# C-B products of a unit in one step, over two PSUM banks, in a fused scan and two-MLP kernel

## The chip, the cores and the metric

The kernel runs on one core of one Trainium2 chip. The metric is the device time of one execution, in microseconds (us). Engines are named as in the profile: PE (TensorE, the matrix engine), DVE (VectorE), ACT (ScalarE), POOL (GpSimd) and SP (the engine whose queue issues the DMAs).

## What is computed

A scan in chunks feeds a first MLP, and that a second one. The scan has 4 batches, 8 heads, 768 steps, head size 32 and state size 16; each MLP takes the 3072 x 256 result as its tokens.

```
for c in range(nc):
    cum = np.cumsum(la, axis=-1)
    L = np.exp(cum[:, :, :, None] - cum[:, :, None, :]) * causal
    CB = np.einsum('bhin,bhjn->bhij', Cc, Bc)
    y_intra = np.einsum('bhij,bhjd->bhid', CB * L, xc)
    y_inter = np.einsum('bhin,bhnd->bhid', Cc, state) * decay_to_i[:, :, :, None]
    y[:, :, sl] = y_intra + y_inter
    state = decay_full[:, :, None, None] * state + np.sum(Bx, axis=2)
x = y as tokens x 256
h = x @ w_in;  g = where(h > 0, h, exp(min(h, 0)) - 1);  x = g @ w_out     (d_ff 2048)
out = ((x @ w_a) * (x @ w_b)) @ w_out                                      (d_ff 1536)
```

## The kernel before

**Units and tiles.** The scan is cut into 24 units (`unit`, L556): one chunk of 128 steps of one batch, all 8 heads. Four units make a tile of 512 tokens; there are six tiles. Units 0 to 3 feed tile 0, units 4 to 7 tile 1, and so on. The first MLP runs tile by tile, in 8 pairs of hidden blocks a tile (`pair`, `down`); the second MLP runs in 18 groups after it (`group`), as products of seven sums over two tiles.

**What a unit does.** DVE turns the decay row into the triangle L by two scans (`scan`, L630), one for each half of the heads. PE makes the C-B products, one 128 x 128 product per head with 16 rows of contraction (`cbm`, L683; for units 0 to 3 `cbm2`, L666). DVE multiplies them into L (`mask`, L686), one instruction per half. PE then makes y (`ym`, L717, L721) and the change of state (L725). ACT and DVE read y out of its bank: `x_hi` and `x_lo` (L760, L763), or `x_w` for tile 0, and `st_up` (L741) for the state.

**How the C-B products stand.** In units 0 to 3 the two halves of the heads lie on two groups of rows of PE (partitions `row` and `row + 32`), in f32; `cbm2` issues all eight products in one step, from one group and the other in turn, and writes into two banks of a ring. Units 4 to 7 have the same f32 data, units 8 to 23 have bf16 data that is cut into three parts and stacked over 128 rows. In units 4 to 23 a unit has two steps of four products, both into the bank `cbank`, so the second waits for the first half's mask:

```
i_cb = add({"PE": 0.28 if s else 0.88}, cbm, cb.take(), i_sm, due=due, ...)
...
i_k = add({"DVE": 0.685}, mask, i_cb, i_scan[g], i_le, due=due)
```

**Banks.** PSUM has eight banks: two for each of the two `up` buffers, two `acc`, `cbank` and `ybank`. `ybank` holds y in columns 0 to 255 and two buffers for the change of state (`dsb`) in 256 to 383. Products on zeros go to 384 to 511.

**What sets the order.** Every piece of work is a step handed to `Plan.add` with its cost on an engine, the steps it follows and a due time. `Plan.emit` (L156 on) walks through them with a clock of its own, takes the step with the earliest start and then the earliest due time, and writes it to its engine's queue. The order on all engines is fixed when the program is made. `MOVE` is a table that shifts due times of single steps by hand. Until 50 us of that clock, where PE would stand still, the planner has `warm` write products on zeros (`plan.fill`, L369) into its queue; below they are called fills.

**Weights.** They come as 64-bit floats and are turned to f32 by ACT, DVE and POOL (`weight`). Tile 0 is multiplied in plain f32 (`whole_mm`, L783); from tile 1 on every operand is split in a high and a low part, with three products for one (L792 to L795, L804 to L808).

Of the kernel before, what the change touches and what calls it, by code (L numbers as in the profile page):

```python
# [17 lines left out]
P = 128  # L18
NB, NH, S, D, N = 4, 8, 768, 32, 16
# [27 lines left out]


MOVE = {
    ("bc", (0, 2, 1)): {"": 3.2, "rest": -2.7},  # L50
    ("bc", (1, 2, 0)): {"rest": 2.4},
    ("late", 1): {"rest": -2.9},
    ("late", 3): {"": -1.4, "comb": 1.7, "high_s": 3.6},
    ("late", 4): {"": 2.6, "high": 2.5},
    ("late", 6): {"": -5.0, "comb": 3.2},
    ("late", 8): {"": -20},
    ("pair", (1, 3)): {"": -2.5},
    ("pair", (3, 3)): {"": -1.3},
    ("pair", (3, 5)): {"": 1.0},
    ("pair", (3, 6)): {"": 0.6},  # L60
    ("pair", (4, 0)): {"": -2.1},
    ("split", ("w_in", 2)): {"": -4.1},
    ("split", ("w_in", 3)): {"": 5.8},
    ("split", ("w_out", 0)): {"high": -1.3},
    ("split", ("w_out", 1)): {"high": 5.2},
    ("split", ("w_out", 3)): {"": -1.3},
    ("unit", 0): {"scan": -2.0},
    ("unit", 1): {"ld_x": 2.0},
    ("unit", 10): {"": 5.1, "ld_x": -0.4, "x_lo": -0.4},
    ("unit", 11): {"st_up": 0.1},  # L70
    ("unit", 12): {"": 7.3, "ld_sm": 1.4, "mask": 4.4},
    ("unit", 13): {"": -3.7},
    ("unit", 14): {"ld_sm": -1.5},
    ("unit", 15): {"": 1.6, "<lambda>": -1.2, "xend": 4.0, "ym": 4.4},
    ("unit", 16): {"cbm": 0.8, "st_bd": 1.3},
    ("unit", 17): {"x_lo": 4.1},
    ("unit", 18): {"<lambda>": -5.5},
    ("unit", 19): {"cbm": 0.5},
    ("unit", 2): {"scan": -0.3},
    ("unit", 20): {"": -4.2, "<lambda>": -1.0, "st_bd": -1.1},  # L80
    ("unit", 21): {"": 7.1, "mask": -5.0, "scan": 2.8},
    ("unit", 22): {"": 2.7, "ld_sm": -1.6, "ld_x": 1.7},
    ("unit", 23): {"": 1.9, "ld_a": 2.0, "scan": 1.7},
    ("unit", 3): {"cbm": 2.6, "last_col": 3.1, "mask": -0.9},
    ("unit", 4): {"": 1.9, "cbm": -3.5, "mask": 0.4},
    ("unit", 5): {"x_lo": -2.4},
    ("unit", 7): {"": 1.6, "ym": -2.8},
    ("unit", 9): {"": -3.0, "st_up": -3.3},
    ("w", ("w_in", 0)): {"sign": -1.0},
    ("w", ("w_in", 2)): {"put": -2.4},  # L90
    ("w", ("w_in", 3)): {"load": -1.7},
    ("w", ("w_out", 1)): {"sign": -0.6},
    ("w", ("w_out", 2)): {"": 2.4},
    ("wb", ("w_a", 0)): {"last3": -1.1},
    ("wb", ("w_a", 1)): {"": 7.0},
    ("wb", ("w_a", 2)): {"load": -5.3, "scale": 3.3, "sign": 0.4},
    ("wb", ("w_b", 2)): {"": 2.4},
    ("wb", ("w_out2", 1)): {"": 3.2, "put": 4.0, "shift": -3.9},
    ("wb", ("w_out2", 2)): {"": 6.1, "shift": 1.8},
    ("xset", 1): {"": 11.1},  # L100
    ("xset", 2): {"": 10.6, "f_t3": -8.8, "x_h": 1.6, "x_l": 6.0},
}


# [133 lines left out]
def kernel(  # L238
# [14 lines left out]
    nc = tc.nc  # L253
# [71 lines left out]
    cbank = psum.tile([P, 4, P], F32, name="cbank", tag="cbank")  # L325
# [3 lines left out]
    cbb, yb = Buf(cbank), Buf(ybank)  # L329
    accb = [Buf(a) for a in accs]  # L330

    def flat4(bf):
        return bf.ap.rearrange("p h i -> p (h i)") if len(bf.ap.shape) == 3 else bf.ap
# [7 lines left out]
    plan = Plan()  # L341
# [214 lines left out]
    def unit(u, due):  # L556
# [82 lines left out]
        if c < NCH - 1:  # L639
# [15 lines left out]
            i_xe = add({"POOL": 0.71}, xend, i_le, i_p, xe.take(), due=due, port=True)  # L655
            xe.users.append(i_xe)
            le.users += [i_le, i_xe]
        i_cbs = None
        if n == 0:

            def cbm2(e):
                for h in range(4):
                    for g in range(2):
                        q = slice(h * P, (h + 1) * P)
                        t = sm32[row + 32 * g:row + 32 * g + N]
                        nc.tensor.matmul(flat4(cb_[g])[:, q], t[:, 0, q], t[:, 1, q], start=True, stop=True)  # L666

            i_cbs = add({"PE": 0.95}, cbm2, cb_[0].take(), cb_[1].take(), i_sm, due=due, weight=0.25)
            smu.users.append(i_cbs)
        for g in range(2):  # L670
            h4 = slice(4 * g, 4 * g + 4)

            cb = cb_[g] if n == 0 else cbb

            def cbm(e, g=g, cbank=cb.ap):
                for h in range(4):
                    if s == 0:
                        q = slice(h * P, (h + 1) * P)
                        t = sm32[row + 32 * g:row + 32 * g + N]
                    else:  # L680
                        q = slice((4 * g + h) * P, (4 * g + h + 1) * P)
                        t = sm.ap
                    nc.tensor.matmul(cbank[:, h, :], t[:, 0, q], t[:, 1, q], start=True, stop=True)  # L683

            def mask(e, h4=h4, cbank=cb.ap if len(cb.ap.shape) == 3 else cb.ap.rearrange("p (h i) -> p h i", h=4)):
                nc.vector.tensor_mul(lt[:, h4], cbank, lt[:, h4])  # L686

            if n:
                i_cb = add({"PE": 0.28 if s else 0.88}, cbm, cb.take(), i_sm, due=due, pad=pd, weight=1.0 if s else 0.125)
                smu.users.append(i_cb)  # L690
            else:
                i_cb = i_cbs
            i_k = add({"DVE": 0.685}, mask, i_cb, i_scan[g], i_le, due=due)
            cb.users += [i_cb, i_k]
            i_msk.append(i_k)
        i_cd = i_sbd = None
        if c > 0:
# [99 lines left out]
    def down(ph, t, f, gh, gl, i_h, i_l, due):  # L797

        name = "w_out" if ph == "A" else "w_out2"
        last = (NA if ph == "A" else NBF) - 1  # L800
        wk = (name, f // 4)

        def hi_mm(m, first):
            nc.tensor.matmul(accs[m], w_mm(name, whi, f, m), gh, start=(f == 0), stop=False)  # L804
            nc.tensor.matmul(accs[m], w_mm(name, wlo, f, m), gh, start=False, stop=False)  # L805

        def lo_mm(m):
            nc.tensor.matmul(accs[m], w_mm(name, whi, f, m), gl, start=False, stop=(f == last))  # L808

        def dn_h(e):  # L810
            hi_mm(0, f == 0)
            hi_mm(1, f == 0)

        def dn_l(e):
            lo_mm(0)
            lo_mm(1)

        def dn_0(e):
            hi_mm(0, False)
            lo_mm(0)  # L820

        def dn_1(e):
            hi_mm(1, False)
            lo_mm(1)

        prev = i_down.get((ph, t))
        d = (accb[0].take() + accb[1].take()) if f == 0 else prev
        if ph == "A" and t == 0:
            i1 = []
            for m in range(2):  # L830
                def dn_w(e, m=m):
                    whole_mm(accs[m], name, f, m, gh, f == 0, f == last)

                i1.append(add({"PE": 0.86}, dn_w, i_h, i_m[wk], d, i1, due=due))
            i_down[ph, t] = i1
            mbuf[wk].users += i1
            return i1, i1
        if f < last:
            i1 = add({"PE": 4 * MM}, dn_h, i_h, i_hi[wk], i_lo[wk], d, due=due)
            i2 = add({"PE": 2 * MM}, dn_l, i_l, i1, due=due)  # L840
            i_down[ph, t] = i2
            w_used[wk] += [i1, i2]
            return [i1, i2], [i2, i2]
        i1 = add({"PE": 3 * MM}, dn_0, i_h, i_l, i_hi[wk], i_lo[wk], d, due=due)
        i2 = add({"PE": 3 * MM}, dn_1, i1, due=due)
        w_used[wk] += [i1, i2]
        return [i1, i2], [i1, i2]

    def pair(t, p):
# [14 lines left out]
        for q, k in ((q, k) for q in range(2 if t == 0 and p < NHALF else 0) for k in range(2)):  # L864

            def up_h(e, k=k, f=2 * p + k, q=q):
                o = slice(q * 256, (q + 1) * 256)
                for c in range(2):
                    whole_mm(u[:, k, o], "w_in", f, c, x0[:, c, o], c == 0, c == 1)

            i_u.append(add({"PE": 0.88}, up_h, d_u, i_u, i_x[t][2 * q:2 * q + 2], i_m["w_in", 0],
                           due=due + 7.0 * q + 0.1 * k))
            mbuf["w_in", 0].users.append(i_u[-1])
        for k in range(0 if t == 0 and p < NHALF else 2):
            f = 2 * p + k

            def up_a(e, k=k, f=f):
                up_mm(u[:, k, :], "w_in", f, t)

            wk = ("w_in", f // 4)  # L880
            if t == 0:
                i_u.append(add({"PE": 1.72}, up_a, d_u, i_u, i_x[t], i_m[wk], due=due + 0.1 * k))
                mbuf[wk].users.append(i_u[-1])
            else:
                i_u.append(add({"PE": 6 * MM}, up_a, d_u, i_u, i_x[t], i_hi[wk], i_lo[wk], due=due + 0.1 * k))
                w_used[wk].append(i_u[-1])
# [551 lines left out]
```

## Time and profile before

| what | value |
|---|---|
| three runs, median | 628.99 us (628.84 to 629.89) |
| the profiled execution, its own time | 627.92 us |
| its span, from the first to the last instruction | 626.2 us |
| PE busy | 619.4 us (99%) |
| DVE, ACT, POOL busy | 392.6, 372.4, 342.8 us |
| moved by DMA | 59.96 MB, mean 96 GB/s |
| TensorE clock granted, mean | 0.998 |

The profile is of one execution. What lies around its span, 1.7 us, is start and end of the program. In its table of f32 products one product in the program is two records in the trace, since PE passes twice; bf16 products and those on split operands have one record. The duration printed for a record on PE contains the way through the array, so records overlap; what a product costs in a full queue is the distance from its start to the next start.

### The profile page before, as it was taken

Reading aid. Unit: us, or ns where it says so; the run is one execution under the profiler, and the core shown is the slowest. Engines: PE = TensorE matmul, PEld = TensorE weight load, DVE = VectorE, ACT = ScalarE, POOL = GpSimd, SP = SyncE. Lnnn points to the kernel's source line nnn. Section 1 sums busy time; section 2 is a strip of 40 time slices with the busy share of each in tenths; the row PEclk is TensorE's granted clock in tenths of the full one; section 3 lists DMA queues with packets and bytes.
Section 4 is the critical chain, followed back from the end, with each engine's and each line's share of the span. In section 5 each row is a group of like instructions: output and inputs, shape, how many; then the busy total and the mean of one; then the engine's idle time right before and its main releaser. Section 6 shows DMA issues by size and latency. Waiting matters only on the chain. (4 is left out here: it accounts for less than half of the span.)

```text
span 626.2 us, 9495 instructions
## 1 busy us (share of the span) xinstructions
PE 619.4 (99%) x3658; PEld 485.3 (77%) x3658; DVE 392.6 (63%) x525; ACT 372.4 (59%) x528; POOL 342.8 (55%) x260
## 2 busy tenths in 40 slices
PE   9999999999999999999999999999999999999997
PEld 8955556788777788777888888888888888788885
DVE  7876686787876987887753766346533446433333
ACT  2375747647676776756678655557544456554443
POOL 2233465246764586546637476557655666555552
PEclk9999999999999999999999999999999999999999
DMA  6968622657668766410000000000100000100001
GB/s 194 337 198 268 208 66 92 223 173 269 214 201 299 269 211 188 152 51 1 1 1 0 2 0 1 0 1 1 68 0 2 2 0 1 68 2 0 1 0 68
DMA packets 33405, 59.96 MB, mean 96 GB/s; under 512 B 2736, under 2 KB 13904, under 8 KB 33360
## 3 DMA queue, kind: packets, MB, share of 16 engines
q1 hardware_dynamic: 33360, 59.35, 28.9%
q8 instruction: 29, 0.48, 0.3%
q14 instruction: 16, 0.13, 0.1%
HBM read 47.61 MB, written 11.73 MB: 95 GB/s over the span
## 5 line engine op out<-in xcount | busy, mean ns | idle before, releaser
L1209 DVE TENSOR_TENSOR x<-x 128x512 f32<-128x512 f32 x36 | 31.7, 884 | 82.5 <-POOL x L1253 82.0
L911 POOL TENSOR_TENSOR gl<-e,gh 128x1024 fp32r<-128x1024 f32 x20 | 50.9, 2545 | 29.1 <-ACT gh L904 21.9
L1215 POOL TENSOR_TENSOR gl<-x,gh 128x512 fp32r<-128x512 f32 x35 | 48.8, 1395 | 32.9 <-ACT gh L1212 32.9
L1253 POOL TENSOR_TENSOR x<-e,x 128x512 f32<-128x512 f32 x36 | 46.3, 1304 | 31.6 <-ACT e L1192 29.4
L804 PE MATMUL acc<-gh,hi_w_out 128*128 128x512 f32 x160 | 63.4, 396 | 0.0
L805 PE MATMUL acc<-gh,lo_w_out 128*128 128x512 f32 x160 | 62.4, 390 | 0.0
L890 ACT ACTIVATE e<-up 128x1024 f32<-128x1024 f32 x44 | 45.1, 1024 | 26.2 <-PE up L795 18.8
L630 DVE TENSOR_TENSOR_SCAN ab<-ab,delta 128x512 f32<-128x512 f32 x36 | 53.6, 1514 | 0.0
L808 PE MATMUL acc<-gl,hi_w_out 128*128 128x512 f32 x160 | 51.3, 397 | 0.1
L894 ACT ACTIVATE e<-e,bias 128x1024 f32<-128x1024 f32 x44 | 50.7, 1153 | 1.0
L900 DVE SCALAR_TENSOR_TENSOR up<-e,up 128x512 f32<-128x512 f32 x40 | 27.7, 692 | 24.8 <-ACT e L894 24.1
L1215 POOL TENSOR_TENSOR gl<-p,gh 128x512 fp32r<-128x512 f32 x18 | 23.9, 1327 | 30.8 <-issue 25.9
L792 PE MATMUL up<-xh,hi_w_in 128*128 128x512 f32 x96 | 39.4, 410 | 0.6 <-DVE gl L909 0.6
L1200 DVE TENSOR_TENSOR p<-acc,p 128x512 f32<-128x512 f32 x36 | 24.6, 690 | 24.5 <-PE acc L1182 23.2
L900 DVE SCALAR_TENSOR_TENSOR e<-e,up 128x512 f32<-128x512 f32 x48 | 30.7, 679 | 11.6 <-ACT e L894 11.4
L1121 PE MATMUL up<-gh,lo_w_out 128*128 128x512 f32 x96 | 37.5, 391 | 0.0
L793 PE MATMUL up<-xh,lo_w_in 128*128 128x512 f32 x96 | 37.5, 390 | 0.0
L1120 PE MATMUL up<-gh,hi_w_out 128*128 128x512 f32 x96 | 37.4, 390 | 0.0
L493 POOL TENSOR_TENSOR m<-m,raw 128x1024 int32<-128x1024 int32 x10 | 26.0, 2605 | 16.9 <-DVE m L483 13.9
L805 PEld LDWEIGHTS acc<-gh,lo_w_out 128*128 128x128 f32 x160 | 30.1, 188 | 5.9
L804 PEld LDWEIGHTS acc<-gh,hi_w_out 128*128 128x128 f32 x160 | 30.0, 188 | 5.9
L686 DVE TENSOR_TENSOR ab<-cbank,ab 128x512 f32<-128x512 f32 x37 | 25.3, 683 | 13.4 <-PE cbank L683 12.6
(306 smaller groups left out, 1731.9 us busy)
## 6 DMA issues: line engine op xcount, KB each, us to landing
ab<-a_seg SPq DMA_DIRECT2D x18, 512.0 KB
parts<-raw SPq DMA_DIRECT2D x64, 128.0 KB
sm<-parts SPq DMA_DIRECT2D x16, 512.0 KB
p<-in_xb SPq DMA_DIRECT2D x20, 256.0 KB
raw<-in_w_out SPq DMA_DIRECT2D x4, 1024.0 KB
fx<-in_w_out SPq DMA_DIRECT2D x3, 1024.0 KB
out_t<-m SPq DMA_DIRECT2D x12, 256.0 KB
raw<-in_w_in SPq DMA_DIRECT2D x2, 1024.0 KB
```

The lines of the kernel that those rows point to most:

```text
L630: nc.vector.tensor_tensor_scan(lt[:, h4].rearrange(flat), lt[:, h4].rearrange(flat) if n else flat4(sp[g]), delta.rearrange(flat), 0.0, op ...
L792: nc.tensor.matmul(ps, w_mm(name, whi, f, c), xh[:, c, :], start=(c == 0), stop=False)
L793: nc.tensor.matmul(ps, w_mm(name, wlo, f, c), xh[:, c, :], start=False, stop=False)
L804: nc.tensor.matmul(accs[m], w_mm(name, whi, f, m), gh, start=(f == 0), stop=False)
L805: nc.tensor.matmul(accs[m], w_mm(name, wlo, f, m), gh, start=False, stop=False)
L808: nc.tensor.matmul(accs[m], w_mm(name, whi, f, m), gl, start=False, stop=(f == last))
L890: nc.scalar.activation(gf, u, AF.Exp)
L894: nc.scalar.activation(gf, gf, AF.Identity, bias=bias[:, 0:1])
L900: nc.vector.scalar_tensor_tensor(u[:, k, :] if on_dve else gf[:, k, :], gf[:, k, :], 0.0, u[:, k, :], op0=ALU.min, op1=ALU.max)
L911: nc.gpsimd.tensor_sub(gl.ap, gf, gh.ap.bitcast(F32))
L1215: eng[e].tensor_sub(tap("l" + w), tap(wa), tap("h" + w).bitcast(F32))
L1253: eng[e].tensor_add(tap(w), tap(v), tap(w))
```

## The change

It touches the C-B products of units 4 to 23, and the due times.

- A unit's eight C-B products become one step. The first half goes to `cbank`, the second to `ybank`, over all its 512 columns. So the step waits until the y, and both buffers of the change of state, of the unit before have been read out.
- Units 4 to 7 now take the form of units 0 to 3 (`cbm2`): products of the two row groups in turn. Units 8 to 23 keep one product after the other, eight in a row (`cbm`).
- Both masks wait for the one step; the second reads `ybank`.
- With unit 4's C-B step the fills end, as `ybank` is no longer free for them.
- `MOVE` is written anew, from 52 to 104 entries, and the planner's costs of the f32 products of tile 0 go up. The costs are seen by the planner alone.

```diff
 MOVE = {
-    ("bc", (0, 2, 1)): {"": 3.2, "rest": -2.7},
...
+    ("bc", (0, 1, 0)): {"": 2.5, "load": 0.9},
...
-        i_cbs = None
-        if n == 0:
-
-            def cbm2(e):
+
+        if n:
+            cb_ = [cbb, yb]
+        cap = [flat4(x) for x in cb_]
+
+        def cbm2(e):
+            if n:
+                plan.fill = None
+            for h in range(4):
+                for g in range(2):
+                    q = slice(h * P, (h + 1) * P)
+                    t = sm32[row + 32 * g:row + 32 * g + N]
+                    nc.tensor.matmul(cap[g][:, q], t[:, 0, q], t[:, 1, q], start=True, stop=True)
+
+        def cbm(e):
+            for g in range(2):
                 for h in range(4):
...
+                    q = slice((4 * g + h) * P, (4 * g + h + 1) * P)
+                    nc.tensor.matmul(cap[g][:, h * P:(h + 1) * P], sm.ap[:, 0, q], sm.ap[:, 1, q], start=True, stop=True)
+
+        old = cb_[0].take() + cb_[1].take() + (dsb[0].users + dsb[1].users if n else [])
+        if s == 0:
+            i_cb = add({"PE": 1.1 if n == 0 else 1.25}, cbm2, old, i_sm, due=due, weight=0.25)
+        else:
+            i_cb = add({"PE": 0.58}, cbm, old, i_sm, due=due, pad=pd)
+        smu.users.append(i_cb)
...
-                i1.append(add({"PE": 0.86}, dn_w, i_h, i_m[wk], d, i1, due=due))
+                i1.append(add({"PE": 0.92}, dn_w, i_h, i_m[wk], d, i1, due=due))
...
-            i_u.append(add({"PE": 0.88}, up_h, d_u, i_u, i_x[t][2 * q:2 * q + 2], i_m["w_in", 0],
+            i_u.append(add({"PE": 0.92}, up_h, d_u, i_u, i_x[t][2 * q:2 * q + 2], i_m["w_in", 0],
...
-                i_u.append(add({"PE": 1.72}, up_a, d_u, i_u, i_x[t], i_m[wk], due=due + 0.1 * k))
+                i_u.append(add({"PE": 1.84}, up_a, d_u, i_u, i_x[t], i_m[wk], due=due + 0.1 * k))
```

How it moves instructions is shown at two places of PE's queue. The first is unit 4, while tile 0 is in the first MLP. Before (`sm_76` holds B and C, `x_93` tile 0, `m_104` and `m_103` weights, `e_86` a result of the hidden layer):

```order
L783 MATMUL up_115<-x_93,m_104 128x512 x2
L683 MATMUL cbank<-sm_76 128x128 x4
L783 MATMUL up_115<-x_93,m_104 128x512 x2
L783 MATMUL acc_117<-e_86,m_103 128x512
L783 MATMUL acc_118<-e_86,m_103 128x512
L717 MATMUL ybank<-p_74,sbd 32x128 x4
L721 MATMUL ybank<-f_hi_w_out_99,p_74 32x128 x4
L717 MATMUL ybank<-p_74,sbd 32x128 x4
L721 MATMUL ybank<-f_hi_w_out_99,p_74 32x128 x4
L725 MATMUL ybank<-xe,p_74 32x64 x4
```

This is unit 4's second half and then its y; the first half stands six products earlier, behind unit 3's y. Now:

```order
L722 MATMUL cbank<-sm_76 128x128
L722 MATMUL ybank<-sm_76 128x128
L722 MATMUL cbank<-sm_76 128x128
L722 MATMUL ybank<-sm_76 128x128
L722 MATMUL cbank<-sm_76 128x128
L722 MATMUL ybank<-sm_76 128x128
L722 MATMUL cbank<-sm_76 128x128
L722 MATMUL ybank<-sm_76 128x128
L832 MATMUL up_115<-x_93,m_104 128x512 x4
L766 MATMUL ybank<-p_74,sbd 32x128 x4
L770 MATMUL ybank<-f_hi_w_out_99,p_74 32x128 x4
```

All eight products stand together, the two banks in turn, four f32 products of the MLP ahead of unit 4's y; where the first half stood, behind unit 3's y, there are now 18 fills.

The second place is unit 8's y in tile 1, still on PE (`gh_90` and `xh_608` are operands of the first MLP). Before:

```order
L717 MATMUL ybank<-p_74,sbd 32x128 x4
L721 MATMUL ybank<-ab_78,p_74 32x128 x4
L725 MATMUL ybank<-xe,p_74 32x64 x4
L683 LDWEIGHTS sm_77
L683 MATMUL cbank<-sm_77 128x128
L683 LDWEIGHTS sm_77
L683 MATMUL cbank<-sm_77 128x128
L683 LDWEIGHTS sm_77
L683 MATMUL cbank<-sm_77 128x128
L683 LDWEIGHTS sm_77
L683 MATMUL cbank<-sm_77 128x128
L804 MATMUL acc_117<-gh_90,hi_w_out_862 128x512
```

Unit 9's first half follows unit 8's y at once; this is so behind 12 of the 16 y steps of units 8 to 23. Now:

```order
L766 MATMUL ybank<-p_74,sbd 32x128 x4
L770 MATMUL ybank<-ab_78,p_74 32x128 x4
L774 MATMUL ybank<-xe,p_74 32x64 x4
L841 MATMUL up_115<-xh_586,hi_w_in_824 128x512
L842 MATMUL up_115<-xh_586,lo_w_in_832 128x512
L841 MATMUL up_115<-xh_586,hi_w_in_824 128x512
L842 MATMUL up_115<-xh_586,lo_w_in_832 128x512
L844 MATMUL up_115<-xl_590,hi_w_in_824 128x512 x2
L853 MATMUL acc_117<-gh_90,hi_w_out_837 128x512
```

Here products of the MLP follow, 16 of 512 columns until unit 9's C-B step. Over the whole program PE has 190 fills before and 176 now; its other products are the same in number.

## Rows read from the trace of the kernel before

**Rows 1.** The page, parts 1 and 2: PE busy (first line), its granted clock in tenths

```profile
PE 619.4 (99%) x3658; PEld 485.3 (77%) x3658; DVE 392.6 (63%) x525; ACT 372.4 (59%) x528; POOL 342.8 (55%) x260
...
PEclk9999999999999999999999999999999999999999
```

**Rows 2.** Who waited for whom, PE: total us, times, longest; without the start

```profile
PE up L792 <- DVE gl L909: 0.6, 1, 0.6
PE up L1124 <- POOL gl L1215: 0.4, 1, 0.4
PE cbank L683 <- DVE ab L686: 0.2, 1, 0.2
```

**Rows 3.** PE's timeline (start us, duration us, engine, line), unit 0's C-B step

```profile
7.29 0.37 PE L666 MATMUL cbank<-sm 16*128 16x128 f32 x1
7.30 0.37 PE L666 MATMUL up<-sm 16*128 16x128 f32 x1
...
8.38 2.05 PE L606 MATMUL acc<-a,delta 128*128 128x128 f32 x16
```

**Rows 4.** PE's timeline around a C-B step of unit 6 and one of unit 7

```profile
61.63 3.60 PE L783 MATMUL up<-x,m 128*128 128x512 f32 x8
65.16 1.15 PE L683 MATMUL cbank<-sm 16*128 16x128 f32 x8
66.24 1.12 PE L783 MATMUL acc<-m,m 128*128 128x512 f32 x2
67.21 1.88 PE L783 MATMUL up<-x,m 128*128 128x512 f32 x4
...
80.11 2.74 PE L783 MATMUL acc<-e,m 128*128 128x512 f32 x6
82.78 1.15 PE L683 MATMUL cbank<-sm 16*128 16x128 f32 x8
```

**Rows 5.** PE's timeline, the longest row of fills, then unit 3's y

```profile
25.52 4.35 PE L369 MATMUL ybank<-zt 128*128 128x128 bf16 x75
29.80 0.65 PE L721 MATMUL ybank<-f_lo_w_out,f_lo_w_out 128*32 128x128 f32 x16
```

**Rows 6.** PE's timeline, a bf16 C-B step behind unit 8's y

```profile
120.82 0.40 PE L683 MATMUL cbank<-sm 128*128 128x128 bf16 x4
121.03 0.48 PE L804 MATMUL acc<-gh,hi_w_out 128*128 128x512 f32 x1
121.34 0.40 PE L805 MATMUL acc<-gh,lo_w_out 128*128 128x512 f32 x1
```

**Rows 7.** Timeline of all engines: unit 8's y step ends and is read out

```profile
120.59 0.29 PE L725 MATMUL ybank<-xe,p 128*32 128x64 f32 x8
...
120.96 0.37 ACT L760 CAST xh<-ybank 128x256 fp32r<-128x256 f32 x1
...
121.36 0.28 DVE L741 SCALAR_TENSOR_TENSOR state<-state,db,ybank 128x64 f32<-128x64 f32 x1
121.56 0.42 DVE L763 TENSOR_TENSOR xl<-ybank,xh 128x256 fp32r<-128x256 f32 x1
...
121.89 0.68 DVE L686 TENSOR_TENSOR ab<-cbank,ab 128x512 f32<-128x512 f32 x1
```

**Rows 8.** Busy time in a stretch: its length, then PE, weight load, DVE, ACT, POOL

```profile
110.00:290.00 180.00, 179.13 (x1395) 142.10 (x1394) 143.02 (x195) 122.74 (x149) 103.50 (x77) 1.00 0.59 195
```

**Rows 9.** PE's timeline around the longest wait

```profile
202.00 0.39 PE L804 MATMUL acc<-gh,hi_w_out 128*128 128x512 f32 x1
202.23 0.39 PE L805 MATMUL acc<-gh,lo_w_out 128*128 128x512 f32 x1
202.46 0.61 PE L808 MATMUL acc<-gl,hi_w_out 128*128 128x512 f32 x2
203.70 0.47 PE L792 MATMUL up<-xh,hi_w_in 128*128 128x512 f32 x1 [0.63 <-DVE gl L909]
```

**Rows 10.** PE's timeline, the first product of tile 1

```profile
92.61 0.79 PE L792 MATMUL up<-xh,hi_w_in 128*128 128x512 f32 x1
```

More of the change, by code (lines that the diff above doesn't have):

```diff
@@ L49 @@
 MOVE = {
-    ("bc", (0, 2, 1)): {"": 3.2, "rest": -2.7},
[L51 to L101, printed above, removed]
[7 rows of a table added]
+    ("group", 10): {"dn_h": -1.9, "mm3": -0.6},
+    ("group", 11): {"": -3.2},
+    ("group", 12): {"dn_l": 3.4, "mm3": 1.3},
+    ("group", 17): {"mm3": -4.2},
+    ("group", 2): {"dn_l": -1.5, "mm3": 2.2},
+    ("group", 4): {"lo": -2.8},
+    ("group", 5): {"": -5.2, "ad": 7.0},
@@ new lines @@
+    ("group", 9): {"": -8.9},
+    ("late", 2): {"": 12.6, "high": 4.0},
+    ("late", 3): {"": 6.7, "comb": -4.6, "high": 9.3},
+    ("late", 4): {"high": -7.5, "rest": -5.3},
+    ("late", 5): {"": -20, "high": 7.7},
+    ("late", 6): {"": -8.9},
+    ("late", 7): {"": 16.7},
+    ("late", 8): {"": -5.4, "high": -5.6},
+    ("pair", (0, 2)): {"em": -4.7},
+    ("pair", (0, 3)): {"dn_w": 4.5, "gg": -10.0},
+    ("pair", (0, 4)): {"": -0.9},
+    ("pair", (0, 7)): {"dn_w": 6.1},
+    ("pair", (1, 0)): {"": -1.5},
@@ new lines @@
+    ("pair", (1, 2)): {"": 3.9, "dn_h": 2.3},
+    ("pair", (1, 3)): {"": 1.2},
+    ("pair", (1, 6)): {"": 2.9},
+    ("pair", (1, 7)): {"up_a": -0.9},
+    ("pair", (2, 0)): {"": 0.7, "gg": 3.7},
+    ("pair", (2, 1)): {"lo": 3.6, "up_a": -4.1},
+    ("pair", (2, 2)): {"": 3.7, "dn_h": -1.4, "dn_l": -4.5, "hi": 1.2, "up_a": -2.7},
+    ("pair", (2, 3)): {"": -1.3, "em": 1.9, "up_a": -3.0},
+    ("pair", (2, 4)): {"dn_l": 4.0},
+    ("pair", (2, 5)): {"": -4.9, "hi": -3.2},
+    ("pair", (2, 6)): {"": -7.9, "up_a": -0.9},
@@ new lines @@
+    ("pair", (2, 7)): {"": 0.7},
+    ("pair", (3, 0)): {"": -0.3, "lo": 5.1},
+    ("pair", (3, 2)): {"": 3.3, "em": 0.3, "up_a": 0.8},
+    ("pair", (3, 3)): {"": -4.6, "dn_l": 1.6},
+    ("pair", (3, 4)): {"up_a": 1.4},
+    ("pair", (3, 5)): {"": -1.9, "dn_h": 8.0},
+    ("pair", (3, 7)): {"dn_l": 3.9, "up_a": 2.9},
+    ("pair", (4, 0)): {"": 9.2},
+    ("pair", (4, 1)): {"lo": -1.4},
+    ("pair", (4, 3)): {"": -15.6},
+    ("pair", (4, 4)): {"": -1.1, "dn_h": -2.2, "dn_l": -0.5},
+    ("pair", (4, 5)): {"": 13.1, "dn_h": -1.2},
@@ new lines @@
+    ("pair", (5, 0)): {"dn_l": 4.4, "up_a": 2.8},
+    ("pair", (5, 2)): {"dn_h": -1.1},
+    ("pair", (5, 3)): {"dn_l": 1.0},
+    ("pair", (5, 4)): {"": 6.3, "dn_l": 2.7, "up_a": 2.2},
+    ("pair", (5, 5)): {"": 0.9, "dn_h": -2.1, "dn_l": 5.5},
+    ("pair", (5, 7)): {"dn_h": -0.2},
+    ("split", ("w_in", 0)): {"": 3.9},
+    ("split", ("w_in", 1)): {"": -4.0, "rest": 3.8},
+    ("split", ("w_in", 2)): {"high": -0.9},
+    ("split", ("w_in", 3)): {"": 6.6, "high": 2.6},
+    ("split", ("w_out", 0)): {"high": 7.8, "rest": 7.2},
@@ new lines @@
+    ("split", ("w_out", 2)): {"": -15.8},
+    ("split", ("w_out", 3)): {"": -3.7, "high": 6.3},
+    ("unit", 0): {"": -10.0, "ld0": 2.0, "ld_x": 9.0, "x_w": 3.5},
+    ("unit", 1): {"": -3.1, "scan": -4.0},
+    ("unit", 11): {"st_up": 1.2},
+    ("unit", 12): {"<lambda>": 8.7, "mask": -15.0},
+    ("unit", 13): {"": -12.8, "<lambda>": 5.6, "scan": 1.4},
+    ("unit", 14): {"": 1.6, "cbm": 5.9, "x_hi": -5.2},
+    ("unit", 15): {"ld_a": -2.0, "ld_x": -0.9, "scan": 5.1, "x_hi": 2.9},
+    ("unit", 16): {"": -6.3, "cbm": 17.1, "last_col": -10.8, "ld_x": 17.3, "xend": -10.4},
@@ new lines @@
+    ("unit", 17): {"": 3.1, "last_col": -20, "ld_a": 14.1, "st_bd": 4.7, "xend": 1.1},
+    ("unit", 18): {"": -1.7, "<lambda>": -5.9, "ld_a": 4.1, "ld_sm": 19.2, "scan": 2.9, "st_bd": 4.4},
+    ("unit", 19): {"": 11.0, "ld_sm": 7.3, "scan": -6.6, "ym": 11.5},
+    ("unit", 2): {"": 12.1},
+    ("unit", 20): {"": -1.8, "mask": 9.6, "scan": -2.0},
+    ("unit", 21): {"": -4.0, "scan": 7.5},
+    ("unit", 22): {"": -1.4, "cbm": 15.5},
+    ("unit", 23): {"": -20},
+    ("unit", 3): {"": 14.9},
+    ("unit", 4): {"": 1.2, "<lambda>": 3.7, "scan": 1.0},
@@ new lines @@
+    ("unit", 5): {"": 0.8, "ld0": 11.2, "ld_a": 2.2, "ld_x": 7.4},
+    ("unit", 6): {"": -8.0, "<lambda>": -9.4, "ld0": 6.3, "ld_a": 4.2, "ld_x": 0.9},
+    ("unit", 7): {"ld_x": -6.1, "st_bd": 8.9},
+    ("unit", 8): {"<lambda>": 19.5, "ld_a": 1.6, "ld_x": 12.9, "scan": 3.6, "st_bd": -9.8},
+    ("unit", 9): {"": -0.4, "st_up": -9.0},
+    ("w", ("w_in", 0)): {"": -2.6},
+    ("w", ("w_in", 1)): {"last3": 2.6, "put": 9.2},
+    ("w", ("w_in", 2)): {"": 2.9, "shift": -4.5},
+    ("w", ("w_in", 3)): {"put": -3.9, "scale": -4.1, "sign": -12.4},
@@ new lines @@
+    ("w", ("w_out", 0)): {"": -13.3},
+    ("w", ("w_out", 1)): {"sign": 1.8},
+    ("w", ("w_out", 2)): {"": -2.4, "load": 3.2},
+    ("w", ("w_out", 3)): {"": 1.8, "shift": 6.3},
+    ("wb", ("w_a", 0)): {"": -3.2, "last3": 7.8},
+    ("wb", ("w_a", 1)): {"load": -6.5},
+    ("wb", ("w_a", 2)): {"": 2.8, "load": 12.6, "sign": 5.2},
+    ("wb", ("w_b", 0)): {"load": -18.5, "scale": -20, "shift": -3.8},
+    ("wb", ("w_b", 1)): {"": 2.8, "last3": 15.1, "shift": 5.3},
+    ("wb", ("w_b", 2)): {"": -6.5, "last3": -3.2, "shift": 6.6, "sign": 4.4},
@@ L102 @@
+    ("wb", ("w_out2", 0)): {"last3": 6.3, "shift": 9.8},
+    ("wb", ("w_out2", 1)): {"": -4.1, "scale": 5.1, "shift": 7.1},
+    ("wb", ("w_out2", 2)): {"": 12.7},
+    ("xset", 1): {"": -3.3},
 }
@@ L657, in unit @@
             le.users += [i_le, i_xe]
-        i_cbs = None
-        if n == 0:
-            def cbm2(e):
-                for h in range(4):
[L663 to L669, printed above, removed]
+        if n:
+            cb_ = [cbb, yb]
@@ L670, in unit @@
+        old = cb_[0].take() + cb_[1].take() + (dsb[0].users + dsb[1].users if n else [])
[4 more added lines that the diff above has]
+        smu.users.append(i_cb)
         for g in range(2):
             h4 = slice(4 * g, 4 * g + 4)
[L673 to L692, printed above, removed]
+            def mask(e, h4=h4, cap=cap[g].rearrange("p (h i) -> p h i", h=4)):
+                nc.vector.tensor_mul(lt[:, h4], cap, lt[:, h4])
@@ L693, in unit @@
             i_k = add({"DVE": 0.685}, mask, i_cb, i_scan[g], i_le, due=due)
-            cb.users += [i_cb, i_k]
+            cb_[g].users += [i_cb, i_k]
             i_msk.append(i_k)
```

6 rows, old and new, of the table MOVE are left out of this document.

## The prediction

> **What bounds the kernel now.** I read the page's busy row and clock row first, then the table of who waited for whom on TensorE (PE), then PE's timeline in the two stretches that the change touches, and last the busy time of the other engines there. PE is busy 619.4 us, 99% of the span, and its clock is at full speed, 2.4 GHz, in all 40 slices [rows 1]. After the start the wait table lists three waits on PE, 0.6, 0.4 and 0.2 us, 1.2 us together [rows 2]. So the time is, within about 1%, the sum of what stands in PE's queue. An edit is worth what it takes out of that queue, unless it makes a new wait; a faster VectorE (DVE), ScalarE (ACT) or GpSimd (POOL) is worth nothing by itself.
>
> **The f32 C-B products (units 4 to 7).** Before, a unit has two steps of four f32 products, each on 16 rows. One such step takes 66.24 - 65.16 = 1.08 us of PE [rows 4]. It also costs something at its edges. Between it and the f32 products of the MLP, eight records take 3.53 us up to a step (61.63 to 65.16) and six take 2.67 (80.11 to 82.78), so a record is 0.43 and the entry 3.53 - 8 x 0.43 = 0.09. The two records behind a step take 67.21 - 66.24 = 0.97, where 0.86 is the norm: the return costs 0.11 [rows 4]. Eight steps, of which the first stands right behind a y step and pays no entry: 8 x 1.08 + 7 x 0.09 + 8 x 0.11 = 10.15 us.
>
> After, a unit has one step of eight products, taken from two groups of rows in turn. The trace has this form already for units 0 to 3: the two groups start 0.01 us apart (7.29 and 7.30), and sixteen records are through 1.09 us after the first (8.38) [rows 3], the same as eight records of one group. Four steps: 4 x (1.09 + 0.09 + 0.11) = 5.16 us. The difference is **-5.0 us**. What no row shows is this pair written into cbank and ybank; in rows 3 it goes to cbank and a bank of up. The ends are 1.09 for the pair, and, if the groups did not overlap, two steps in a row, 2.16, with which the part would be worth -5.0 + 4 x 1.07 = -0.7. I take 1.09: same instructions, same two row groups, two different banks in both.
>
> **The fill products.** The planner puts products on zeros into PE's queue where its own clock expects a gap. They are real work: 75 of them take 29.80 - 25.52 = 4.28 us, 0.057 each [rows 5]. Counted in the order there are 190 before and 176 after. 14 x 0.057 = **-0.8 us**. The last 12 before stand behind unit 4's first C-B step, where the new program has no filler any more; the 18 new ones behind unit 3's y step take the place of that C-B step. The ends are -0.8 and 0, the latter if PE just waits where it was filled; I take -0.8 because the steps that follow had room: unit 3's y step waits for a scan and two masks that hang on PE's own spread step, and that moves forward with the fills that are gone ahead of it.
>
> **The bf16 C-B products (units 8 to 23).** A step of four takes 121.03 - 120.82 = 0.21 us, and the product behind it 121.34 - 121.03 = 0.31 where 0.23 is usual, a return of 0.08 [rows 6]. Before: 32 steps, 16 y steps, and in the order 12 C-B steps stand right behind a y step, which makes one return of two. 32 x 0.21 + 36 x 0.08 = 9.60. After: 16 steps of eight; a further four of 128 columns in a row are 4 x 0.057 (the fills have the same shape, rows 5), so 0.44 a step. No C-B step can stand behind a y step now, as it needs y's bank empty, so 32 returns: 16 x 0.44 + 32 x 0.08 = 9.60. **0.0 us**: what is saved in steps is lost in neighbours.
>
> **What is moved.** All other steps keep their number (apart from the fills PE's queue has the same products, SP the same 213 DMAs) and are put in another order by the new due times. The raised planner costs (0.86 to 0.92 and so on) only move steps too. On SP the loads of the first MLP's weights keep their sequence among each other, with one load of decay rows put ahead of the fifth; loads of x and decay shift by a few places. I take the reordering at 0. What hides it is the slack of the other engines: DVE is busy 143.02 of the 180 us from 110 to 290, ACT 122.74, POOL 103.50 [rows 8]. The ends: -1.2 if all listed waits go [rows 2], +3.1 if four more come of the size of the largest (two products from 202.46 on, the next at 203.70: 1.24 us for two spacings that are 0.23 each elsewhere in rows 9, so 0.78 lost) [rows 9]. What is late next, once PE runs 5.8 us ahead, is the first product of tile 1, which needs the y of unit 7 evicted; in the new order 11 f32 products (9.4 us at 2 x 0.43) stand between the two, before it was 6.
>
> **The new wait.** From unit 4 on, a C-B step needs both cbank and ybank, and what waits there has all of PE's queue behind it. y's bank is free when ACT's high copy and DVE's state and low steps are done: the last piece of a y step starts at 120.59 and ends 0.23 later, the low step ends at 121.56 + 0.42 = 121.98, 1.16 us behind the y step [rows 7]. In the new order at least 10 products of 512 columns, 10 x 0.23 = 2.3 us, stand between any y step and the next C-B step of units 9 to 23. Behind a C-B step y needs two masks of 0.68 [rows 7], and at least 12 products, 2.8 us, are there. I cost the wait at 0. If DVE were more than 1.1 us late with one of them, PE would wait by the excess.
>
> The TensorEngine Tiling (Array Packing) page of the Trainium skill (Restrictions and Gotchas, PSUM Pressure) speaks against the change here: different row tiles write to different PSUM banks, so the pairing is paid for with a second bank, and with the synchronisation for it. Rows 3 agree as far as the two banks go; no row shows y's bank used so. By that rule the outcome would lean to the second rival below, whose price is from rows 7 to 9.
>
> **Sum.** -5.0 - 0.8 + 0.0 + 0 = -5.8 us. The profiled execution took 627.92 us, so 622.1 for one like it; it was 1.07 below the median of 628.99, so the **forecast is 623.2 us**. (About 0.2% of this kernel, 1.3 us, is what a measurement can tell from no change.)
>
> **Rivals.**
> 1. The waits go too. The due times are set anew for the whole program, and the three waits are at single places [rows 2]. Against it: the old due times had the same purpose and left them. 623.2 - 1.2 = 622.0; chance 0.2.
> 2. Slower: y's bank becomes the bound. The step chain C-B, masks, y, eviction now runs through one bank per unit, with DVE 79% busy [rows 8] and in-order. It decides from 5.8 / 16 = 0.36 us of extra wait per unit. At the size of rows 9, 0.78 in each of 16 units, +12.5: 635.7 us. Against it are the 1.1 us of room worked out above; chance 0.04.
> 3. PE outruns the others: with PE 5.8 us ahead, DVE, whose work is the same, comes late a few more times between 110 and 290 us, four more waits of 0.78, 3.1 us: 626.3 us. For it: all three waits are on results of DVE or POOL already [rows 2]; chance 0.16.
> 4. The change doesn't do what it says: the two groups follow each other in cbank and ybank, and the fills that go leave waits. 628.99 - 0.7 = 628.3; chance 0.05.
>
> **How the numbers follow.** The forecast has 0.55. The range reaches down to the first rival and a little of the fills' edges, 621.2, and up to the third, 626.6; outside are 2, 4 and tails. Faster by over 0.2% (below 627.7) are the forecast and rivals 1 and 3, 0.91; within 0.2% is most of rival 4, 0.05; slower is rival 2, 0.04.
>
> **What would show it.** In the changed kernel's profile: records of units 4 to 7 in cbank and ybank starting 0.01 us apart, and a step through in 1.09 us; four such steps between 30 and 85 us where there were eight; 176 fills; the first product with the high half of w_in on tile 1 near 86.8 us instead of 92.61 [rows 10]; PE still 99% busy; waits of PE on ybank or cbank below 0.5 us in all. A group of PE waits on DVE's or ACT's reading of ybank, one per unit, would prove rival 2; a step of 2.1 us, rival 4; a tile 1 that starts 5.8 us early with an end that is only 3 early, rival 3.

## The result, and the profile after

The changed kernel takes **622.84 us** (median of four runs, 622.29 to 624.13), the kernel before 629.12 (628.84 to 629.89): ratio 0.9901, 95% interval 0.9883 to 0.9919. Run again beside later experiments it took 623.80 us (five runs, 623.57 to 624.41), the kernel before 628.77 there: 0.9921, 0.9909 to 0.9932. The forecast of 623.2 us lies between the two medians. The profiled execution took 622.29 us, its span is 620.6.

The page of the changed kernel answers to [rows 1]: PE is still busy 99%, and for 5.6 us less, which is the change of the span.

```profile
PE 613.8 (99%) x3644; PEld 480.7 (77%) x3644; DVE 394.1 (64%) x526; ACT 373.0 (60%) x527; POOL 344.5 (56%) x260
...
PEclk9999999999999999999999999999999999999999
```

Who waited for whom, PE, answers to [rows 2]. The first of those rows of before (0.6 on gl) and the last (0.2 on ab) are gone, and a 0.6 on ACT's reading of y (x, L806) and a 0.2 on ACT's raw (L583) are new; the 1.1 is the start, which [rows 2] leaves out. No row names a C-B step, line L722 or L728:

```profile
PE ybank L421 <- POOL zt L417: 1.1, 1, 1.1
PE ybank L421 <- ACT x L806: 0.6, 1, 0.6
PE up L1173 <- POOL gl L1264: 0.3, 1, 0.3
PE up L841 <- ACT raw L583: 0.2, 1, 0.2
```

PE's timeline around the joint step of unit 7 (columns as in [rows 4]):

```profile
69.68 1.02 PE L832 MATMUL acc<-f_lo_w_in,m 128*128 128x512 f32 x2
70.63 0.37 PE L722 MATMUL cbank<-sm 16*128 16x128 f32 x1
70.64 0.37 PE L722 MATMUL ybank<-sm 16*128 16x128 f32 x1
...
71.72 1.55 PE L832 MATMUL up<-x,m 128*128 128x512 f32 x3
```

The two groups start 0.01 us apart and are through in 71.72 - 70.63 = 1.09; all four steps of units 4 to 7 (from 35.34, 44.81, 60.30 and 70.63) take the same. The entry is 0.95 - 2 x 0.43 = 0.09. A joint bf16 step, unit 9's, answers to [rows 6]:

```profile
117.03 0.40 PE L728 MATMUL cbank<-sm 128*128 128x128 bf16 x4
117.26 0.39 PE L728 MATMUL ybank<-sm 128*128 128x128 bf16 x4
117.46 0.71 PE L857 MATMUL acc<-gl,hi_w_out 128*128 128x512 f32 x2
```

It takes 117.46 - 117.03 = 0.43, as do the other 15. Last, the stretch behind unit 3's y, and the first product of tile 1, which answers to [rows 10]:

```profile
28.13 0.29 PE L774 MATMUL ybank<-xe,f_lo_w_out 128*32 128x64 f32 x8
29.03 1.17 PE L421 MATMUL ybank<-zt 128*128 128x128 bf16 x18 [0.60 <-ACT x L806]
30.03 5.38 PE L832 MATMUL up<-x,m 128*128 128x256 f32 x16
...
86.48 0.79 PE L841 MATMUL up<-xh,hi_w_in 128*128 128x512 f32 x1
```

**Where the time went.** PE runs nearly without a gap, so four marks in its queue split the time: the start of unit 0's C-B step, the first product of tile 1, the 1200th product from the end, and the start of the last one. The third mark lies between 337 and 348 us in all kernels, where the last products of the first MLP mix with the first of the second; from there on all kernels have 1200 products of 512 columns.

| from mark to mark, us | before | after | after, again |
|---|---|---|---|
| start to unit 0's C-B step | 7.29 | 6.24 | 7.26 |
| to the first product of tile 1 | 85.31 | 80.23 | 80.23 |
| to the 1200th product from the end | 253.35 | 253.18 | 253.39 |
| to the last product | 275.47 | 276.13 | 276.18 |

The 5.64 us of the profiled pair are -1.05 -5.08 -0.17 +0.66. The first is luck: the instructions ahead of unit 0's step are the same, and in the second profile of the same kernel it is gone (last section); over the twelve profiles of all kernels here that step starts between 6.10 and 7.29 us. What belongs to the change is -4.6 in the first profile and -4.3 in the second. The -5.08 comes back in both to 0.01 us. The +0.66 behind the third mark is waits: before had one long one there (0.83 us between two products from 532.35), after has three (0.74 from 361.68, 0.51 from 405.61, 0.40 from 533.77). Neither the new steps nor the new due times make them alone: with one of the two changed the last stretch is 275.53 and 275.10 (below). It is the order that both make together.

### The profile page after: what moved, and what is told of

The parts are those of the page before. It is cut to its first block, busy times and chain, and to the rows that moved or that the text cites. A ratio compares the mean times of both kernels' runs of the same rounds, so it can differ in the third digit from the quotient of the medians.

```text
span 620.6 us, 9487 instructions
## 1 busy us (share of the span) xinstructions
PE 613.8 (99%) x3644; PEld 480.7 (77%) x3644; DVE 394.1 (64%) x526; ACT 373.0 (60%) x527; POOL 344.5 (56%) x260
## 4 chain that ended last, share of the span: by engine, by line
PE 91%; POOL 3%; DMA 2%; DVE 2%; ACT 1%; issue 1%; SPq 0%; POOLq 0%; DVEq 0%; ACTq 0%
PE acc L853 5%; PE up L841 5%; PE acc L857 5%; PE acc L854 5%; PE up L842 5%; PE up L844 5%; PE up L1173 5%; PE up L1169 5%; PE up L1170 5%; PE up L832 5%; PE acc L832 5%; PE acc L1230 4%; PE acc L1229 4%; PE acc L1231 4%; PE ybank L1230 3%; PE ybank L1229 3%
## 5 line engine op out<-in xcount | busy, mean ns | idle before, releaser
L960 POOL TENSOR_TENSOR gl<-e,gh 128x1024 fp32r<-128x1024 f32 x20 | 53.4, 2669 | 30.1 <-ACT gh L953 28.6
L1261 ACT CAST gh<-x 128x512 fp32r<-128x512 f32 x36 | 22.4, 622 | 21.9 <-DVE x L1258 21.7
```

Source lines behind the costliest of these rows:

```text
L960: nc.gpsimd.tensor_sub(gl.ap, gf, gh.ap.bitcast(F32))
```

## The experiments

Two theories. **A**, the prediction's: the time is PE's queue; the pairing of row groups takes out 5.0 us and the fills 0.8, the bf16 steps and the new order nothing. **B**: the new order does it, and the pairing matters little. Times of runs are medians; "first stretch" is the second row of the table above, which does not contain the luck at the start, "middle" its third row and "last stretch" its fourth.

### The pairing alone

One group after the other, in the same joint step, for units 4 to 7:

```diff
-            for h in range(4):
-                for g in range(2):
+            for h, g in ([(h, g) for g in range(2) for h in range(4)] if n else [(h, g) for h in range(4) for g in range(2)]):
+                if True:
```

> The changed kernel, with the eight f32 products of units 4 to 7 in another order inside their step: four of the first row group, then four of the second. Nothing else moves on any engine. Theory A (the gain is PE time saved by the two row groups running side by side): four steps go from 1.09 to about 2.16 us each, so 4.3 us slower than the changed kernel, 627.1 us, 0.997 of the kernel before. Theory B (the gain comes from the new order of the whole program): within 1 us of the changed kernel, 622 to 624. In the profile, the step of unit 4 would take 2.16 us by A and 1.1 by B.

Measured 625.93 us (625.00 to 626.17), 3.1 above the changed kernel's first median and 2.1 above its second. The first stretch is 82.42, so +2.19. Neither number was expected, and unit 4's step shows why:

```profile
36.07 0.82 PE L722 MATMUL cbank<-sm 16*128 16x128 f32 x5
36.62 0.37 PE L722 MATMUL ybank<-sm 16*128 16x128 f32 x1
...
37.06 0.72 PE L722 MATMUL ybank<-sm 16*128 16x128 f32 x5
37.70 1.13 PE L832 MATMUL up<-x,m 128*128 128x512 f32 x2
```

The second group does not wait for the end of the first: it starts 0.55 us behind it, beside its fifth record of eight, and the step takes 37.70 - 36.07 = 1.64 and not 2.16. Four steps x 0.55 = 2.2 us, the whole of the difference in the stretch. So the alternation is worth 2.2 us over eight products in a row; the rest of the gain on these steps comes from joining them.

### Old steps with the new due times, new steps with the old ones

The first is the kernel before with the new `MOVE` and the new planner costs, the second the changed kernel with the old `MOVE`.

> The kernel before, with the due times and planner costs of the changed one, and its own C-B steps. Theory A: the f32 steps stay at eight of 1.08 us, 173 fills instead of 190 take off 1.0, and waits come in because the due times were made for other steps: 628 to 632 us. Theory B: most of the 6.3 us, 623 to 625.

> The changed kernel with the due times of the kernel before. Theory A: the 5.0 us of the f32 products and 0.8 of the fills are there, less what waits cost with due times that were made for other steps: 623 to 627 us. Theory B: near the kernel before, 628 to 632.

The new steps with old due times took 623.86 us (623.50 to 624.60), with a ratio to before of 0.9922 (0.9910 to 0.9934), which can't be told from the changed kernel's two, 0.9901 and 0.9921; the first stretch is 80.33. **So the steps carry the gain**, as A says. The due times only move waits here: in the middle it lost 1.95 us against the changed kernel (255.13), most of it at one C-B step whose data came late, and it won 0.60 back behind the third mark (275.53):

```profile
193.09 0.40 PE L676 MATMUL cbank<-sm 128*128 128x128 bf16 x4 [2.04 <-DMA sm<-parts]
```

Old steps with new due times took 626.34 us (626.23 to 626.76), 2.7 less than before, where A expected no gain. Its profile shows 1.7 of them: 0.74 is the start (unit 0's step at 6.55), which is luck, 1.20 the first stretch (84.11), where 17 fills fewer are 0.9; the middle (253.96) gives 0.6 back and the end (275.10) wins 0.4. The profiled execution of before was 1.1 us below the median of its runs, this one 0.1 below, so the other 1.0 us is in executions without a profile. About 1.0 of the 2.7 us is thus traced to the order and its fills, and where the rest lies stays open. The two trials, 5.2 and 2.7 us faster than before, do not add up to the 5.0 to 6.3 of the changed kernel either.

### The bf16 steps

The changed kernel with two steps of four for units 8 to 23, both into `cbank`:

```diff
+        if s:
+            cb_ = [cbb, cbb]
...
+                i_cb = add({"PE": 0.28}, cbm, cbb.take(), i_sm, due=due, pad=pd)
```

> The changed kernel, but units 8 to 23 with two steps of four products into cbank, as before; units 4 to 7 as changed; due times of the changed kernel. Theory A with a bf16 term of 0.0: 622 to 625 us, the difference to the changed kernel being waits alone. Theory C (one step over two banks for the bf16 units is a part of the gain): 2 us or more slower than the changed kernel without more waits of PE. Theory D (the new claim on the bank of y costs time in the changed kernel): faster than the changed kernel, by up to 1 us.

Measured 626.38 us (12 runs, 624.65 to 628.91), 2.6 to 3.5 slower. The first stretch is 80.23 again; the loss is in the middle, 257.68 against 253.18, and by waits, while the last stretch wins 1.0 (275.16):

```profile
PE cbank L741 <- DVE ab L735: 1.7, 2, 1.4
PE up L844 <- DVE gl L961: 1.5, 1, 1.5
PE ybank L421 <- POOL zt L417: 1.1, 1, 1.1
PE acc L860 <- POOL gl L963: 1.0, 1, 1.0
```

The two waits of a C-B step for a mask, 1.7 us, are what a single bank does: the second half can't be written before DVE has masked the first. That needs DVE to be late, and before the longer one, which ends at 199.65, it was: weights for the second MLP came in late there (DVE waited 1.70 us at 190.92 for `raw`), and the waits on gl, made by DVE and POOL from then on, are most likely its followers, which is argued and not shown. The medians hold something more: six of the twelve executions have a mean granted clock of 0.993 to 0.997 and took 626.57 to 628.91 us, the other six, with the profiled one, have 0.998 to 1.000 and took 624.65 to 626.19. Theory A (622 to 625) fell as far as it said that nothing hangs on the second bank. Is that a gain over the kernel before, then? The opposite trial is the kernel before with the bf16 steps joined. Its edit also raises the planner's costs as in the changed kernel, which the expectation does not name:

> The kernel before, with its due times, units 4 to 7 as before (two f32 steps each into cbank), and only the bf16 products of units 8 to 23 joined into one step of eight, the second half in y's bank. Theory A, the prediction's: worth 0.0 by spacings and no new wait: 628 to 630 us. Theory C, the second bank frees the second half from the masks of the first, which is what the run with two bf16 steps in the new order lost 5 us on: some of the waits near 188 and 202 us go, 0.3 to 1.5 us faster, 627.5 to 628.5. Theory D, the joint step has to wait for y's bank: slower than 630, with waits of PE on ybank or cbank.

Measured 629.22 us (628.12 to 631.54) against 628.77, ratio 1.0008, 0.9998 to 1.0018: no gain there as a whole. But its first stretch, which has no bf16 step in it, is 86.30 against 85.31: the raised costs put unit 4's first step into another place (last experiment). So that joining the bf16 steps is worth 0.0, as predicted, fits the run and is not shown by it; without the 0.99 it would be some 0.5 us faster than before by the medians. Its profile has one wait of the kind that the second rival was made of, a step that found y's bank not read out:

```profile
194.84 0.40 PE L677 MATMUL cbank<-sm 128*128 128x128 bf16 x4
196.29 0.38 PE L677 MATMUL ybank<-sm 128*128 128x128 bf16 x4 [1.05 <-DVE xl L771]
```

It stands in the same stretch, where DVE is late. So both forms wait there, for a mask or for y, and which of them costs less depends on the order around it.

### The fills

The changed kernel with 32 fills fewer (the 18 behind unit 3's y, and 7 each of the blocks of 51 and 72), and with none after the first 31. The planner counts them all as before, so no other instruction changes its place:

```diff
+    emitted = [2, 12, 17, 4, 44, 65, 0]
...
-        for _ in range(n):
+        for _ in range(emitted.pop(0)):
```

> The changed kernel with 32 of its 176 fills left out (the last block of 18 goes, 7 each leave the blocks of 51 and 72); the planner still counts them, so the order of all other products is the same. Theory A, fills that PE runs after its next work is ready lie on the path: in the changed kernel ACT ends reading y of unit 3 at 28.98, the 18 fills run from 29.03 to 30.03 and only then come f32 products that wait for nothing, so 1.0 to 1.6 us go there, and up to 0.4 at each of the other two blocks: 620.8 to 621.9 us. Theory B, PE would only wait where it was filled (the end of 0 that the prediction gave to its term on the fills): within 0.4 of the changed kernel, 622.4 to 623.2.

> The changed kernel with only the first 31 fills; the other 145 are left out, the order of all other products is the same. Theory A, the fills cover gaps and cost time where they are too many: 620.8 to 622.0 us, and the granted clock stays at 2.4 GHz. Theory B, the fills keep the clock up: with gaps in their place PE's records between 10 and 30 us run at 1.2 GHz, products of 128 columns at twice 0.057 us and f32 products of 512 columns at twice 0.43 until the clock rises again, 3 us or more in all: 625 us or more.

> The changed kernel itself, unaltered, on the same chip as the three others, to compare them with. 622 to 624 us. Its first C-B step shows whether the 1.05 us by which that step came earlier in the changed kernel's profile (6.24 against 7.29, behind the same instructions) belongs to the kernel (again 6.2 to 6.3) or to the execution (anywhere between 6.2 and 7.3).

With fewer fills 621.55 us (620.78 to 622.21), ratio 0.9883, interval 0.9869 to 0.9897, which does not touch that of the changed kernel on the same chip (0.9909 to 0.9932). In a second set of runs, below, 621.34. The first stretch was 79.19 in its profile, where a late load made unit 1's C-B step 1.74 us long instead of 1.09, and 78.50 in the second: 80.23 - 78.50 = 1.73 us for 32 fills, 0.054 each, where fills start 0.056 apart. **All 32 were on the path**, within 0.1 us. This version is 2.25 us faster than the changed kernel on the same chip, of which the stretch shows 1.7.

With none after the first 31, 624.47 us (623.70 to 628.28). PE then stands still twice for over 2 us, and the first f32 products behind the gap are slow. PE's timeline and its windows (length; busy us of PE, its weight load, DVE, ACT, POOL; granted clock; DMA):

```profile
18.92 3.60 PE L834 MATMUL up<-x,m 128*128 128x256 f32 x8 [2.30 <-DVE le L701]
```

```profile
16.00:18.00 2.00, 0.62 (x6) 0.43 (x4) 2.00 (x3) 0.02 (x1) 0.00 (x0) 1.00 1.04 422
18.00:19.00 1.00, 0.08 (x1) 0.11 (x1) 1.00 (x3) 1.00 (x1) 0.00 (x0) 0.91 1.02 418
19.00:20.00 1.00, 1.00 (x3) 0.82 (x4) 1.00 (x2) 1.00 (x2) 0.62 (x1) 0.50 1.01 414
20.00:22.00 2.00, 2.00 (x6) 1.59 (x5) 1.97 (x4) 1.26 (x2) 0.00 (x0) 0.50 1.09 242
...
27.70:29.00 1.30, 0.96 (x24) 0.56 (x24) 1.30 (x3) 0.10 (x1) 0.07 (x1) 1.00 0.96 321
29.00:29.40 0.40, 0.00 (x0) 0.00 (x0) 0.40 (x1) 0.39 (x2) 0.00 (x0) 0.57 0.98 399
```

The same eight records print 1.95 us in the changed kernel (from 18.91) and 3.60 here: the granted clock behind the gap is 0.50, the lower of the two levels, 1.2 GHz. It is so again from 30 to 32 us, where sixteen records print 6.91 instead of 5.38. There a wait of 2.37 us ends at 27.75 and unit 3's y runs, for which the clock row still has 1.00; the clock falls in the wait of 0.61 us behind it. Three of the eight executions have a mean clock of 0.986 to 0.988 and took 626.96 to 628.28 us; the other five have 0.993 to 0.995 and took 623.70 to 624.89. So both theories were half right: the fills keep the clock up, and those that outlast the wait they fill are paid for in full.

### The place behind unit 3's y

What remained open was why the first stretch gained 5.08 and not 5.0 + 0.8. In the kernel before, unit 4's first C-B step stood behind unit 3's y [rows 5], ten products of the MLP and 12 fills ahead of its second (not six products, as said above); in the changed kernel fills stand there, which first wait 0.6 us. This run puts unit 4's joint step back into that place, in the kernel with fewer fills:

```diff
+        if u == 4:
+            cap[1] = flat4(accb[0])
...
+                    if w == (("unit", 3), "ym"):
+                        self.steps[self.parts.index((("unit", 4), "cbm2"))][1]("PE")
```

> The kernel of the run with fewer fills, and in it unit 4's joint C-B step put where the kernel before had unit 4's first one, right behind unit 3's y (its load of B and C ahead of the load of its decay rows, its second half into an acc bank that is free there, not into y's). All else keeps its order. Theory A: at this place PE has nothing to do until ACT has read y, 0.90 us from the last product group of y to the next f32 product in the run with fewer fills, while the kernel before, with a step of 1.08 there, took 1.31; so a step here costs 0.4 and not 1.2, and one of the eight steps that the prediction took off the path had been mostly off it already. With the joint step there the place takes 1.3 us again and 1.29 us go at its old place: from unit 0's C-B step to the first product of tile 1 78.3 us, where the run with fewer fills took 79.2 (0.2 of it a late load): 0.6 to 0.9 us less. Theory B: PE's gap there is not ACT's reading, or the step is held up by its load: 79.2 or more.

> The kernel with 32 fills fewer once more, unaltered, to compare the run above with on the same chip: 621 to 622.3 us; from unit 0's C-B step to the first product of tile 1 79.0 to 79.2 us.

With the step there, then without it:

```profile
27.92 0.29 PE L784 MATMUL ybank<-xe,f_lo_w_out 128*32 128x64 f32 x8
28.15 0.37 PE L732 MATMUL cbank<-sm 16*128 16x128 f32 x1
...
29.24 1.78 PE L842 MATMUL up<-x,m 128*128 128x256 f32 x7
```

```profile
27.24 0.29 PE L776 MATMUL ybank<-xe,f_lo_w_out 128*32 128x64 f32 x8
28.14 2.42 PE L834 MATMUL up<-x,m 128*128 128x256 f32 x9 [0.61 <-ACT x L808]
```

The place takes 29.24 - 27.92 = 1.32 us with a step in it and 28.14 - 27.24 = 0.90 without: the step costs 0.42 there, as theory A said, since PE has to wait for ACT in any case. The first stretch is 78.14 against 78.50, 0.36 less instead of the expected 0.6 to 0.9, because products that now come earlier wait for DVE (0.27 us at 34.94, none there without the move). The medians, 621.79 (620.37 to 622.33) and 621.34 (620.42 to 622.10), can't be told apart, so as a version it is no better.

The kernel before with the bf16 steps joined shows the same from the other side. There unit 4's first step, an old one of four products, runs ahead of unit 3's y, and the place behind that y holds nothing but fills, which wait for ACT:

```profile
28.10 1.15 PE L697 MATMUL cbank<-sm 16*128 16x128 f32 x8
...
29.65 0.29 PE L733 MATMUL ybank<-xe,f_lo_w_out 128*32 128x64 f32 x8
30.55 1.17 PE L369 MATMUL ybank<-zt 128*128 128x128 bf16 x18 [0.60 <-ACT x L765]
```

With the same f32 steps as before and one fill less, its first stretch is 0.99 us longer; a step that leaves the shadow costs 1.19 - 0.42 = 0.77 of that, the rest is open.

## Why the prediction was right, step by step

- **What bounds the kernel.** Right. PE stays 99% busy, and the 5.64 us between the two profiles are found in its queue.
- **The f32 products, -5.0.** The prices were right: step 1.09, entry 0.09, four steps. But the first of the eight old steps was taken off the path at its full 1.08 + 0.11, and it had stood where PE waits for ACT's reading of unit 3's y. A step there costs 0.42. This is the sentence that failed: that the first step "stands right behind a y step and pays no entry" was seen, and not that it paid only part of the rest. The term is nearer to -5.0 + 1.19 - 0.42 = -4.2; the first stretch, with the fills taken off, gives -4.3.
- **The fills, -0.8.** 14 fewer at the 0.054 us that the trimmed run gives are -0.76, as said; no run takes these 14 alone away. The reason given, that the steps that follow had room, held for 32 more in the changed kernel.
- **The bf16 steps, 0.0.** Right by spacing (0.43 against the estimate of 0.44); the run with these joined in the old order fits it and does not show it, since its first stretch moved too. That nothing would hang on the second bank was wrong for the new order, where two steps in one bank lost 4.5 us in the middle and won 1.0 behind it.
- **The new order, 0.** The sum of the last two stretches is +0.5 us in the first profile and +0.75 in the second, within the ends of -1.2 and +3.1. Two of the three listed waits went and others came in the second MLP, so neither the first rival (all go) nor the third (four more between 110 and 290) describes it.
- **The new wait, 0.** Right for all 20 joint steps; none waits for y or a mask. The sign set for it, waits on ybank or cbank below 0.5 us in all, was missed all the same, by the 0.6 us of the fills behind unit 3's y.
- **Sum.** Forecast -5.8 for the pair of executions, measured -5.64, of which 1.05 is the start. Without that it is -4.6 and -4.3, 1.2 to 1.5 us less than forecast: 0.7 is what the first stretch lacks, the shadow of that first step by its size, and 0.5 to 0.75 the order. That the median came out so near is in part luck: the kernel's first set of runs was the faster one; by the second set (-5.0) the gain was over-estimated by 0.8.
- **The rivals.** The fourth (groups not side by side) would not have given 628.3 even where it holds: written one after the other the two groups still overlap, and a step is 1.64, not 2.16. The second's kind of wait exists, once, in the old order with the bf16 steps joined; it needs DVE to be late for another reason.

By the Trainium skill's TensorEngine Tiling (Array Packing) page (Restrictions and Gotchas, PSUM Pressure) different row tiles write to different PSUM banks, and software must keep them in step. The trace agrees on the banks, cbank and ybank in all four f32 steps; the lean to the second rival that the prediction took from it did not come, with no wait at any joint step. What the second bank cost here was the one place behind unit 3's y, where y's bank was not free for the joint step.

## What to carry to other kernels

Before an instruction that goes is counted at its full length, look at what stands behind it and whether that could start any earlier: a step in the shadow of another engine's work is worth only the part that sticks out, here 0.4 of 1.2 us. Products that only keep an engine busy should end with the wait they cover; compare the end of the last real releaser with the start of the next real product, and cut by the difference, but not to nothing where the clock depends on them. And compare two profiles of one kernel before a difference of 1 us near the start is put down to a change.

## What the runs showed of the hardware that was not expected

- **The clock at the start rises at different moments, and the clock row does not show it.** PE's timeline of the start, before:

```profile
3.92 0.64 PE L369 MATMUL ybank<-zt 128*128 128x128 bf16 x4
4.34 2.46 PE L606 MATMUL acc<-a,delta 128*128 128x128 f32 x11
```

  and after:

```profile
3.91 0.56 PE L421 MATMUL ybank<-zt 128*128 128x128 bf16 x4
4.31 2.00 PE L658 MATMUL acc<-a,delta 128*128 128x128 f32 x16
```

  The fills up to 4.2 us start 0.107 us apart, nearly twice the 0.056 of later ones, in both. The spread products then start 0.214 apart until 6.4 us in before and in the second profile of after, and 0.111 apart from 4.5 us on in the first. By these distances PE ran at 1.2 GHz for about 2 us longer in two of the executions, while the clock row gives full speed from the first slice on.
- **Products of two row groups overlap even when written one group after the other**, from the fifth of eight records on (36.07 and 36.62 us, unit 4). They wrote into two banks; one bank for both was not tried.
- **The granted clock fell to 0.50 around PE's waits in one kernel and not in two others.** With no fills after the first 31 it fell at the end of a wait of 2.30 us (0.91 on average from 18 to 19 us), and again behind one of 2.37, in the next wait of 0.61. In the changed kernel waits of 0.60 us at that second place left it at 1.00, and so did a wait of 2.04 us in the middle of the new steps with old due times:

```profile
191.00:193.00 2.00, 0.05 (x1) 0.00 (x0) 1.14 (x2) 1.65 (x2) 0.00 (x0) 1.00 1.03 387
193.00:194.00 1.00, 0.91 (x10) 0.87 (x11) 0.97 (x2) 1.00 (x2) 0.00 (x0) 1.00 1.03 414
```

  What sets these cases apart was not tried.
